# Two of VectorE's three exponential patterns, summed by accumulating DMAs and multiplied once

## The chip, the core and the metric

The kernel runs on one core of a Trainium2 chip. TensorE (PE), ScalarE (ACT), VectorE (DVE), GpSimd (POOL) and SyncE (SP) each work through an instruction list of their own, in order, and wait for one another by semaphores. The metric is the device time of one execution in microseconds, 644.52 for the kernel before (median of 3 runs, 644.18 to 644.57).

## What is computed

Two attention blocks over 2048 positions of width 512, with 32 heads of 16. Block A is linear attention, block B softmax attention; their outputs stand side by side.

```
# A
pq, pk = phi(q), phi(k)              # phi(t) = where(t > 0, t + 1, exp(t)) + 1e-6
num = pq @ (pk^T v);  den = pq @ sum(pk)
a = (num / den) @ wo
# B
p = softmax(q k^T / 4)               # per head, 2048 x 2048
b = (p @ v) @ wo
out = concatenate([a, b], axis=-1)
```

Nearly all the work is B's: 32 heads times 2048 x 2048 exponentials.

## The kernel before

**Tiling.** B goes in 32 *units*: four groups of eight heads (`Gp`), four chunks of 512 queries (`c`), two parities (`e_`), with four heads (`g`) in each unit. A unit has 64 *blocks*; a block is one head, 128 keys (`j`) and 512 queries. For each block TensorE makes the scores (`qk`, L946; four heads share the array, 32 rows each), an engine makes the exponentials, and TensorE multiplies them with V and a column of ones (`pv_cand`, L1355; four heads share the array, 32 columns each) into one PSUM bank per unit. The last unit does the same in halves of 256 queries (L943, L1348). Then VectorE transposes and normalizes (L1394 to L1410) and the output projection follows.

**Two ways to an exponential.** Most blocks go to ScalarE: two or three blocks of scores lie in the PSUM tile pS and one activation (L1161) writes them as f16 into PT, 25 slots. The other blocks lie in single banks of pD, pPV or pS, and VectorE turns them into f16 bit patterns with one multiply and add that writes int16 (L1065): the integer is read as an f16 and grows like the exponential, in straight pieces. To even out the pieces three such patterns are used, the second and third being the first plus 328 and plus 656. GpSimd makes those two with one integer add each (L1245) over a *group* of two blocks. The first pattern is multiplied with VX, which is V times 1.5547, the other two with VV, which is V: three PV products for a block of VectorE's, against one for a block of ScalarE's.

**Buffers.** The patterns lie in `DI`: 8 buffers (`NDG`), each for one group, with its three patterns one behind the other. A buffer comes free when all PV products of its group are done (`dgleft`, `dgfree`).

**What sets the order.** The program is written by a planner that runs while the kernel is built: it keeps a modelled time for each engine, lists of what may start, and picks the next instruction by start time and priority. `d_pick` chooses blocks for VectorE, `chain` hands a full group to GpSimd, `pv_cand` collects ready products into batches, and jobs of block A and the projections (L636, L735 and others) are put in between. A table `SEG` changes the planner's numbers about every 12 us of its own time, among them a seed for its choices among equals. On the chip only the order is left, with a semaphore wait wherever one instruction needs another's result or its buffer. So TensorE's next score product stands behind every PV product that the planner put ahead of it.

`Sched.add` records an instruction with what it reads and writes and derives its waits; a DMA has a lane (a semaphore) of its own and is issued by the queue that it is given, in that engine's order. A DMA also waits for the one before it on its lane.

Of the kernel before, what the change touches and what calls it, by code (L numbers as in the profile page):

```python
# [10 lines left out]
F16 = mybir.dt.float16  # L11
I16 = mybir.dt.int16
# [227 lines left out]
def bass_concat_heads__linear_attn_block__softmax_full_mha__prompt_kernel(nc, A_x, A_wqkv, A_wo, B_x, B_wqkv, B_wo, out):  # L240
# [8 lines left out]
    LAY = (25, 8)  # L249
    PW = 0.5  # L250
# [6 lines left out]
    NDG = LAY[1]  # L257
# [105 lines left out]
    JB = True  # L363
    WARM = (30, 6)
    HQ = 7.5
    TRACE = None
    PEB = 14


# [1433 lines left out]
```

## Time and profile before

| | |
|---|---|
| runs, median (lowest, highest) | 644.52 us (644.18, 644.57) |
| the profiled execution | 644.23 us |
| its span, first to last instruction | 642.5 us |
| TensorE clock granted | 0.998 |
| ScalarE, 655 exponentials | 615.4 us busy |
| VectorE, 722 pattern instructions, 723 blocks | 193.5 + 159.1 + 135.0 us busy |
| GpSimd, 726 integer adds | 433.2 us busy |
| DMA, all queues | 21.80 MB, 34 GB/s over the span |

The span is one execution as the profiler saw it. A line of the page names the source line, the engine, the operation, the tile written and the tiles read, then the count, the busy time and the mean length of one. The lengths of neighbours overlap on every engine, since a record ends when the result has been written and the next instruction starts before that; for the pace of an engine compare starts. PEld are the weight loads of the matmuls. A wait names who waited and whose instruction ended the wait.

### The profile page before, as it was taken

The numbers are of one execution on the slowest core, as the hardware profiler recorded it, in microseconds if no ns is written. First come the engines' busy times: TensorE is split into PE (matmuls) and PEld (weight loads), VectorE is DVE, ScalarE is ACT, GpSimd is POOL, SyncE is SP. The second block draws the span as 40 slices with busy tenths as digits, with TensorE's granted clock in tenths as the row PEclk, the third lists the DMA queues.
The fourth block names the chain that finished last, engine by engine and source line by source line (L and its number), as shares of the span: only waits on it lengthen the run. The fifth ranks groups of instructions, "written<-read, shape, count | busy, mean of one in ns | idle before, by whom it ended". The sixth has DMA issues, their size and how long they took to land.

```text
span 642.5 us, 20026 instructions
## 1 busy us (share of the span) xinstructions
PE 635.4 (99%) x8562; PEld 218.1 (34%) x8562; DVE 612.0 (95%) x1086; ACT 628.7 (98%) x692; POOL 440.5 (69%) x751
## 2 busy tenths in 40 slices
PE   8999999999999999999999999999999999999997
PEld 6333332333333333343333333223222322223243
DVE  6999999999999999999999999999999999999985
ACT  6999999999999999999999999999999999999995
POOL 4666788876767766657767676677776668766751
PEclk9999999999999999999999999999999999999999
DMA  9701000002010011012021012002110110000112
GB/s 187 209 2 24 21 1 12 8 3 43 3 35 1 2 35 35 10 35 45 18 50 51 3 41 45 17 10 50 28 34 10 27 34 18 26 11 26 35 43 71
DMA packets 53230, 21.80 MB, mean 34 GB/s; under 512 B 44176, under 2 KB 52624, under 8 KB 53136
## 3 DMA queue, kind: packets, MB, share of 16 engines
q1 hardware_dynamic: 51664, 19.80, 13.3%
q8 instruction: 69, 1.13, 0.7%
q10 hardware_dynamic: 1472, 0.66, 0.4%
q14 instruction: 25, 0.20, 0.1%
HBM read 4.46 MB, written 4.19 MB: 13 GB/s over the span
## 4 chain that ended last, share of the span: by engine, by line
PE 68%; ACT 31%; DVE 1%; issue 0%
ACT PT L1161 30%; PE pS L946 22%; PE pD L1355 20%; PE pD L636 7%; PE pPV L1355 4%; PE pS L636 4%; PE pPV L636 3%; PE pD L735 1%; PE pS L943 1%; ACT EA L751 1%; PE pD L946 1%; PE pD L1479 1%; PE pS L735 1%; PE pPV L946 0%; PE pD L1348 0%; PE pPV L1348 0%
## 5 line engine op out<-in xcount | busy, mean ns | idle before, releaser
L1161 ACT ACTIVATE PT<-pS 128x1024 f16<-128x1024 f32 (+1 forms) x655 | 615.4, 1082 | 1.3 <-PE pS L946 1.0
L1245 POOL INT64_ADD DI<-DI x726 | 433.2, 610 | 187.5 <-DVE DI L1065 184.2
L946 PE MATMUL pS<-QT,KM 32*128 32x512 bf16 x1512 | 255.1, 384 | 1.4 <-ACT PT L1161 0.5
L1065 DVE TENSOR_SCALAR DI<-pD 128x512 int16<-128x512 f32 (+1 forms) x288 | 193.5, 681 | 6.9 <-PE pD L946 2.1
L1355 PE MATMUL pD<-PT,VV 128*17 128x512 f16 x979 | 178.0, 381 | 0.0
L1355 PE MATMUL pD<-DI,VV 128*17 128x512 f16 x1114 | 176.8, 381 | 0.0
L1065 DVE TENSOR_SCALAR DI<-pS 128x512 int16<-128x512 f32 x235 | 159.1, 677 | 2.1 <-PE pS L946 1.3
L946 PEld LDWEIGHTS pS<-QT,KM 32*128 32x128 bf16 x1512 | 65.2, 91 | 231.3 <-ACT PT L1161 191.9
L1065 DVE TENSOR_SCALAR DI<-pPV 128x512 int16<-128x512 f32 x199 | 135.0, 678 | 4.6 <-PE pPV L946 2.5
L1355 PE MATMUL pD<-DI,VX 128*17 128x512 f16 x557 | 129.2, 382 | 0.0
L946 PE MATMUL pD<-QT,KM 32*128 32x512 bf16 x275 | 102.8, 384 | 0.0
L946 PE MATMUL pPV<-QT,KM 32*128 32x512 bf16 x197 | 75.7, 384 | 0.0
L1355 PE MATMUL pPV<-PT,VV 128*17 128x512 f16 x299 | 52.0, 381 | 0.0
L1355 PEld LDWEIGHTS pD<-DI,VV 128*17 128x17 bf16 x1114 | 38.9, 88 | 33.6 <-issue 22.3
L1355 PEld LDWEIGHTS pD<-PT,VV 128*17 128x17 bf16 x979 | 39.0, 88 | 30.5 <-issue 24.9
L1355 PE MATMUL pPV<-DI,VV 128*17 128x512 f16 x298 | 49.3, 381 | 0.0
L1355 PEld LDWEIGHTS pD<-DI,VX 128*17 128x17 bf16 x557 | 28.5, 88 | 17.9 <-issue 14.4
L1355 PE MATMUL pPV<-DI,VX 128*17 128x512 f16 x149 | 34.2, 382 | 0.0
L946 PEld LDWEIGHTS pD<-QT,KM 32*128 32x128 bf16 x275 | 24.3, 90 | 1.9 <-DVE DI L1065 0.7
L946 PEld LDWEIGHTS pPV<-QT,KM 32*128 32x128 bf16 x197 | 17.8, 90 | 1.9 <-DVE DI L1065 1.4
L636 PE MATMUL pD<-Wa,xTa 128*32 128x256 bf16 x448 | 18.1, 275 | 0.0
L636 PE MATMUL pS<-Wa,xTa 128*32 128x256 bf16 x448 | 18.0, 275 | 0.0
(202 smaller groups left out, 534.1 us busy)
## 6 DMA issues: line engine op xcount, KB each, us to landing
out_dram<-KNa SPq DMA_DIRECT2D x31, 128.0 KB, 1.8
Wa<-in_A_wqkv_dram SPq DMA_DIRECT2D x1, 1536.0 KB, 8.7
KM<-KR SPq DMA_DIRECT2D x96, 16.0 KB, 1.8
Wb<-in_B_wqkv_dram SPq DMA_DIRECT2D x2, 384.0 KB, 5.6
Wb<-in_B_wqkv_dram SPq DMA_DIRECT2D x1, 512.0 KB, 4.6
Wa<-in_A_wo_dram SPq DMA_DIRECT2D x1, 512.0 KB, 4.4
Wa<-in_B_wo_dram SPq DMA_DIRECT2D x1, 512.0 KB, 3.7
ON<-in_B_x_dram ACTq DMA_DIRECT2D x1, 256.0 KB, 2.8
```

The source lines that it names most:

```text
L636: ins = self.e.matmul(out_[32 * g:32 * g + 32], lhsT=lhsT[:, 32 * g:32 * g + 32], rhs=rhs, start=start, stop=stop, tile_position=(0, 32 * g))
L735: return e.matmul(f32v(bk)[:, tl * 128:(tl + 1) * 128], lhsT=xTb[:, cc, t * 128:(t + 1) * 128], rhs=Wb[:, cc, 1024 + Gp * 128:1024 + Gp * ...
L751: ("act", 0.0635 + n * 0.000833, f_ev("act", lambda e, bk: e.activation(EA[:, 0:n], f32v(bk)[:, c0:c0 + n], ACTF.Exp), [], ["EA"])),
L943: ins = e.matmul(dst[:, 256 * i:256 * i + 256], lhsT=KM[32 * g:32 * g + 32, Gp % 2, e_, (2 * jp + i) * 128:(2 * jp + i + 1) * 128], rhs=QT ...
L946: return e.matmul(dst, lhsT=KM[32 * g:32 * g + 32, Gp % 2, e_, j * 128:(j + 1) * 128], rhs=QT[32 * g:32 * g + 32, Gp % 2, c * 512:(c + 1) ...
L1065: sch.add("dve", lambda e, db_=DBANK[b0]: e.tensor_scalar(DI[:, di_at(0, buf) + i * 512:di_at(0, buf) + (i + n) * 512], f32v(db_, n * 512) ...
L1161: sch.add("act", lambda e: e.activation(PTf[:, p0 * 512:p0 * 512 + w], S5[:, c0:c0 + w], ACTF.Exp, scale=SC), reads=skeys(sl, len(bl)), wr ...
L1245: sch.add("pool", lambda e, v=v, word=word: e.int64_add(at64(v), at64(0), word), reads=keys, writes=[("DI", v, x) for x in best])
L1355: sch.add("pe", lambda e, g=g, j=j, c0=c0, V_=V_, r2=r2, P=P, first=first, last_=last_, pb_=pvb[0]: e.matmul(pb_[0][32 * g:32 * g + 17, pb ...
L1479: ins = e.matmul(f32v(wb_, 128), lhsT=ZW[:], rhs=ZW[:], start=True, stop=True)
```

## The change

It has four parts.

1. After GpSimd's two adds a DMA issued by GpSimd adds the third pattern onto the second, as f16 (`accum_op=ALU.add`). The sum is multiplied with VV once, so a block of VectorE's takes two PV products. A group is left as it was, with three products, when the planner's GpSimd backlog is too long or the last unit is near its end (`joined`). There are 273 such DMAs: 197 over one group (two blocks) and 76 over two groups (four blocks), on six lanes in turn.
2. The three patterns lie in three planes with slots of their own, 9, 9 and 6, 24 as before. A slot of the first plane comes free after its VX products and GpSimd's adds, one of the third when the DMA has landed.
3. GpSimd may join two groups in one add (and one DMA) whatever their slots. The way by which VectorE made the later patterns itself in the last unit is gone.
4. The table `SEG` is new, so all orders are new.

The core of the diff:

```diff
-    LAY = (25, 8)
-    PW = 0.5
+    LAY = (25, (9, 9, 6))
+    PW = 0.8
...
-        (12.0,0.05,5,3.0,0,2,6,4,9.5,26,2.5,7.0,0.8,1.8,3,7.0,1.5,2.5,1.5,3,1,0.3,6,0,-9.0,2,1.2,0,55),
+        (12.1089,0.05,5,3.0,0,2,6,4,9.5,26,2.5,7.0,0.8,1.8,3,7.0,1.5,2.5,1.5,3,1,0.3,6,0,-9.0,2,1.2,0,55),
...
+    PDM = 6.0
+    DMT = 30
+    PDF = 0.58
+    PDG = 0.4
+    SDL = 2.0
+    SDB = 0.00137
+    SDM = 1.3
+    NSL = 6
...
-        DIR = 3 * DGW
-        DI = sb("DI", [128, NDG * DIR], I16)
+        DI = sb("DI", [128, sum(NPL) * DGW], I16)
 
         def di_at(v, b):
 
-            return b * DIR + v * DGW
+            return (sum(NPL[:v]) + b) * DGW
...
+        def plane_hold(v, b, n):
+
+            pfree[v][b] = None
+            pusers[v][b] += n
+
+        def plane_done(v, b, t):
+
+            pusers[v][b] -= 1
+            plast[v][b] = max(plast[v][b], t)
+            if pusers[v][b] == 0:
+                pfree[v][b] = plast[v][b]
+                plast[v][b] = 0.0
...
+        sum_lanes = [sch.new_dma_lane() for _ in range(NSL)]
...
+                joined = p_backlog(st_) < PDM and not (u_min(items) == NU - 1 and left[NU - 1] < DMT)
+                for v in (1, 2):
+                    for x in slots[v]:
+                        plane_hold(v, x, 1 if joined and v == 2 else n)
                     word = int.from_bytes(struct.pack("<4H", *[SHIFT[v - 1]] * 4), "little")
-                    sch.add("pool", lambda e, v=v, word=word: e.int64_add(at64(v), at64(0), word), reads=keys, writes=[("DI", v, x) for x in best])
+                    sch.add("pool", lambda e, v=v, word=word: e.int64_add(at64(v), at64(0), word), reads=keys, writes=[("DI", v, x) for x in slots[v]])
                     T["pool"] = st_ = st_ + PFX + len(best) * w * PEL
...
+                if joined:
+                    lane = sum_lanes[nsum[0] % len(sum_lanes)]
+                    nsum[0] += 1
+                    sch.add(lane, lambda e: e.dma_start(at16(1), at16(2), accum_op=ALU.add), reads=[("DI", 2, x) for x in slots[2]], writes=[("DI", 1, x) for x in slots[1]], queue="pool")
+                    T["pool"] = st_ + PDF + (len(best) - 1) * PDG
+                    sum_end[0] = max(st_ + SDL, sum_end[0]) + len(best) * w * SDB
+                    land = sum_end[0] + SDM
+                    for x, it in zip(slots[1], items):
+                        for b in it:
+                            pv_due[b[0]][b[2]] -= 1
+                            if b[0] == LU:
+                                half_due[b[1] // 8][b[2]] -= 1
+                        give(x, it, 1, land)
+                    for x in slots[2]:
+                        plane_done(2, x, land)
```

In the lines of the kernel after, L953 is the score product, L1401 the PV product, L1195 the exponential, L1096 VectorE's pattern, L1277 the integer add and L1287 the accumulating DMA.

What moves, first on GpSimd. These are its rows before, from the end of the start-up work on; an ISA row is an integer add, its 128x512 are 1024 int16 of two blocks.

```order
L532 AFFINE_SELECT BMk<-BMk 128x128
L547 MEMSET VNa 128x32
L1245 ISA DI<-DI 128x512 x510
L1245 ISA DI<-DI 128x256 x2
L1245 ISA DI<-DI 128x512 x6
```

And these are its rows now, from the middle of the program, with what each waits for: s_dve is VectorE's semaphore, s_pool GpSimd's own, s_d29 and the like are lanes of the accumulating DMAs.

```order
L1277 ISA DI<-DI 128x2x512
L1287 DMA DI<-DI 128x2x1024 [waits s_pool]
L1277 ISA DI<-DI 128x1024 [waits s_dve]
L1277 ISA DI<-DI 128x1024 [waits s_d34,s_d29]
L1287 DMA DI<-DI 128x2048 [waits s_pool]
L1277 ISA DI<-DI 128x512 [waits s_dve]
L1277 ISA DI<-DI 128x512 [waits s_d30]
L1287 DMA DI<-DI 128x1024 [waits s_pool]
```

A DMA stands behind each pair of adds and waits for them; the second add of a pair, into the third plane, waits for an earlier DMA to have landed. Pairs over two groups stand among those over one.

On TensorE, in the seventeenth unit, this is a batch of PV products before, with the score products and half a V projection (L735) behind it; DI,VX is a first pattern, DI,VV a second or third, PT a block of ScalarE's.

```order
L1355 MATMUL pPV<-DI,VV 17x512 x4
L1355 MATMUL pPV<-PT,VV 17x512
L1355 MATMUL pPV<-DI,VX 17x512
L1355 MATMUL pPV<-PT,VV 17x512 x2
L946 MATMUL pS<-QT,KM 128x512 x2
L946 MATMUL pD<-QT,KM 128x512
L735 MATMUL pS<-Wb,xTb 128x128 x8
```

And this stands near the start of the same unit now.

```order
L953 MATMUL pPV<-QT,KM 128x512
L1401 MATMUL pD<-DI,VX 17x512 x2
L1401 MATMUL pD<-PT,VV 17x512 x2
L953 MATMUL pS<-QT,KM 128x512 x2
L953 MATMUL pD<-QT,KM 128x512
L1401 MATMUL pD<-PT,VV 17x512
L1401 MATMUL pD<-DI,VV 17x512 x3
```

The unit has 110 PV products before and 88 now, its batches are shorter, and of DI,VV there is one for a block instead of two.

More of the change, by code (lines that the diff above doesn't have):

```diff
@@ L256, in bass_concat_heads__linear_attn_block__softmax_full_mha__prompt_kernel @@
     DG = 2
-    NDG = LAY[1]
+    NPL = LAY[1]
     VW = 1.5546875
@@ L978, in bass_concat_heads__linear_attn_block__softmax_full_mha__prompt_kernel, with plane_pick, plane_gate @@
         dgroup = {"n": 0, "buf": 0, "open": False}
-        dgfree = [0.0] * NDG
-        dgleft = [0] * NDG
+        pfree = [[0.0] * n for n in NPL]
+        dgfree = pfree[0]
+        pusers = [[0] * n for n in NPL]
+        plast = [[0.0] * n for n in NPL]
+        def plane_hold(v, b, n):
[7 more added lines that the diff above has]
+                plast[v][b] = 0.0
+        def plane_pick(v, n, t):
+            fr = sorted((x, b) for b, x in enumerate(pfree[v]) if x is not None)[:n]
+            return sorted(b for x, b in fr) if len(fr) == n and fr[-1][0] <= t else None
+        def plane_gate():
+            g = [min((x for x in pfree[v] if x is not None), default=None) for v in (1, 2)]
+            return None if None in g else max(g)
         def cur_unit():
@@ L1016, in d_pick @@
             if not dgroup["open"]:
-                buf = min((i for i in range(NDG) if dgfree[i] is not None), key=lambda i: (dgfree[i] > at, (i - dgroup["buf"] - 1) % NDG), default=None)
+                buf = min((i for i in range(NPL[0]) if dgfree[i] is not None), key=lambda i: (dgfree[i] > at, (i - dgroup["buf"] - 1) % NPL[0]), default=None)
                 if buf is None or dgfree[buf] > at:
@@ L1033, in d_take @@
                 dgroup["n"] += 1
-                dgfree[buf] = None
-                dgleft[buf] = 0
+                plane_hold(0, buf, 1)
                 dgroup["st"][buf] = {"taken": 0, "closed": False, "items": []}
@@ L1038, in d_take @@
             s_["taken"] += 1
-            dgleft[buf] += 3
+            plane_hold(0, buf, 1)
             if s_["taken"] == DG:
@@ L1072, in p1 @@
                         dfree[x] = en_ + LPE["dve"]
-                        pv_ready[b_[0]].append((en_ + LPE["dve"], b_, (DI.bitcast(F16)[:, di_at(0, buf) + k_ * 512:di_at(0, buf) + (k_ + 1) * 512], ("DI", 0, buf, k_)), ("d", buf), "X"))
+                        pv_ready[b_[0]].append((en_ + LPE["dve"], b_, (DI.bitcast(F16)[:, di_at(0, buf) + k_ * 512:di_at(0, buf) + (k_ + 1) * 512], ("DI", 0, buf, k_)), ("d", 0, buf), "X"))
                     s_["t"] = en_
@@ L1079, in bass_concat_heads__linear_attn_block__softmax_full_mha__prompt_kernel @@
         pshift = []
+        nsum, sum_end = [0], [0.0]
+        sum_lanes = [sch.new_dma_lane() for _ in range(NSL)]
+        DF = DI.bitcast(F16)
         pv_give = {}
@@ L1203, in chain, with give @@
             s_["chained"] = True
-            late = left[NU - 1] < DE3 and all(b[0] == NU - 1 for b in s_["items"])
             n = len(s_["items"])
             w = 512 * n
-            rk = [("DI", 0, buf, i) for i in range(n)]
-            def give(buf_, v, lane, en_):
-                for i, b in enumerate(dgroup["st"][buf_]["items"]):
-                    P = DI.bitcast(F16)[:, di_at(v, buf_) + i * 512:di_at(v, buf_) + (i + 1) * 512]
-                    pv_ready[b[0]].append((en_ + (LPE["pool"] if lane == "pool" else LPE["dve"]), b, (P, ("DI", v, buf_)), ("d", buf_), "V"))
-            def plain(v):
-                def run(st_, en_):
-                    sch.add("dve", lambda e: e.tensor_scalar(DI[:, di_at(v, buf):di_at(v, buf) + w], DI[:, di_at(0, buf):di_at(0, buf) + w], 1.0, float(SHIFT[v - 1]), op0=ALU.mult, op1=ALU.add),
-                            reads=rk, writes=[("DI", v, buf)])
-                    give(buf, v, "plain", en_)
-                return run
+            def give(slot, items, v, t):
+                for i, b in enumerate(items):
+                    P = DI.bitcast(F16)[:, di_at(v, slot) + i * 512:di_at(v, slot) + (i + 1) * 512]
+                    pv_ready[b[0]].append((t, b, (P, ("DI", v, slot)), ("d", v, slot), "V"))
             def on_pool(st_, en_):
-                near_ = {x[1]: x for x in pshift if x[2] == w and x[3][0] <= st_ + PMW}
+                near_ = {x[0]: x for x in pshift if x[1] == w and x[2][0] <= st_ + PMW}
                 near_[buf] = me[0]
                 best = [buf]
-                for step in range(1, NDG):
-                    run_ = [buf]
-                    while len(run_) < JN and run_[-1] + step in near_:
-                        run_.append(run_[-1] + step)
-                    while len(run_) < JN and run_[0] - step in near_:
-                        run_.insert(0, run_[0] - step)
-                    if len(run_) > len(best):
-                        best = run_
-                keys = []
+                for b2 in sorted(near_, key=lambda b2: near_[b2][2][0]):
+                    if b2 != buf and len(best) < JN and plane_pick(1, 2, st_) and plane_pick(2, 2, st_):
+                        best = sorted((buf, b2))
+                keys, items = [], []
                 for b_ in best:
@@ L1237, in on_pool @@
                     if b_ != buf:
-                        cands["pool"].remove(x[3])
-                        st_ = max(st_, x[3][0])
+                        cands["pool"].remove(x[2])
+                        st_ = max(st_, x[2][0])
                     keys += [("DI", 0, b_, i) for i in range(n)]
-                at64 = lambda v: bass.AP(DW, DW[:, di_at(v, best[0]) // 4:].offset, [list(DW[:, 0:1].ap[0])] +
-                                         ([[(best[1] - best[0]) * DIR // 4, len(best)]] if len(best) > 1 else []) + [[1, w // 4]])
@@ L1243, in on_pool, with at64, at16 @@
-                for v in vs:
+                    items.append(dgroup["st"][b_]["items"])
+                slots = [best] + [plane_pick(v, len(best), st_) for v in (1, 2)]
+                def at64(v):
+                    sl = slots[v]
+                    return bass.AP(DW, DW[:, di_at(v, sl[0]) // 4:].offset, [list(DW[:, 0:1].ap[0])] +
+                                   ([[(sl[1] - sl[0]) * DGW // 4, 2]] if len(sl) > 1 else []) + [[1, w // 4]])
+                def at16(v):
+                    sl = slots[v]
+                    return bass.AP(DF, DF[:, di_at(v, sl[0]):].offset, [list(DF[:, 0:1].ap[0])] + ([[(sl[1] - sl[0]) * DGW, 2]] if len(sl) > 1 else []) + [[1, w]])
@@ L1246, in on_pool @@
                     T["pool"] = st_ = st_ + PFX + len(best) * w * PEL
-                    for x in best:
-                        pv_give[x, v](st_)
-            vs = (1, 2)
-            if late:
-                for v in vs:
-                    push("dve", s_["t"], -2, 0.06 + w * 0.00027, plain(v))
-                return
-            for v in vs:
-                pv_give[buf, v] = lambda en_, v=v: give(buf, v, "pool", en_)
-            me = [(vs, buf, w, push("pool", s_["t"] + LTO["dve", "pool"], 0, len(vs) * (PFX + w * PEL), on_pool), rk)]
+                    if not joined:
+                        for x, it in zip(slots[v], items):
+                            give(x, it, v, st_ + LPE["pool"])
@@ new lines, in on_pool @@
+                for x in best:
+                    plane_done(0, x, st_ + LPE["pool"])
+                if joined:
[13 more added lines that the diff above has]
+                        plane_done(2, x, land)
@@ L1257, in chain, with u_min @@
+            def u_min(items):
+                return min(b[0] for it in items for b in it)
+            me = [(buf, w, push("pool", s_["t"] + LTO["dve", "pool"], 0, 2 * (PFX + w * PEL), on_pool))]
             pshift.append(me[0])
@@ L1362, in run @@
                     if src[0] == "d":
-                        dgleft[src[1]] -= 1
-                        if dgleft[src[1]] == 0 and dgroup["st"][src[1]]["closed"]:
-                            dgfree[src[1]] = en
+                        plane_done(src[1], src[2], en)
                     else:
@@ L1639, in bass_concat_heads__linear_attn_block__softmax_full_mha__prompt_kernel @@
             opts = []
+            gate = plane_gate()
             for eng in T:
                 best = None
+                if eng == "pool" and gate is None:
+                    continue
                 for c_ in cands[eng]:
-                    st = max(pe_at("v" if isinstance(c_[3], Rounds) else "j") if eng == "pe" else T[eng], c_[0])
+                    st = max(pe_at("v" if isinstance(c_[3], Rounds) else "j") if eng == "pe" else T[eng], c_[0], gate if eng == "pool" else 0.0)
                     k_ = (round(st / 0.05), c_[1], c_[2])
```

104 rows, old and new, of the table SEG are left out of this document.

## The prediction

> **What bounds the kernel now.** I read the page first, for the load of each engine and the chain, then the waits, then ScalarE's timeline, and last one late step of it.
>
> ```profile
> span 642.5 us, 20026 instructions
> PE 635.4 (99%) x8562; PEld 218.1 (34%) x8562; DVE 612.0 (95%) x1086; ACT 628.7 (98%) x692; POOL 440.5 (69%) x751
> PE 68%; ACT 31%; DVE 1%; issue 0%
> ```
>
> Three engines look full, and the chain goes through TensorE and ScalarE alone. The profiled execution took 644.23 us, 1.73 more than its span; the median of the runs, 644.52, lies 0.29 above it. A step that I cost at x us in the span I take off the median as it stands.
>
> ```profile
> PEld pS L946 <- ACT PT L1161: 191.9, 481, 0.6
> POOL DI L1245 <- DVE DI L1065: 184.2, 220, 5.3
> PEld pD L1355 <- POOL DI L1245: 5.5, 23, 0.4
> ```
>
> The columns are us in total, times, longest. A fill of the score banks pS (L946) waits for ScalarE to have read a bank 481 times. There are 655 exponentials, so in some 174 cases the bank was free and TensorE came later. GpSimd mostly waits for work, and TensorE hardly waits for GpSimd. "Busy" hides the rest: an exponential is recorded for 1072 ns, but the next starts before it ends. So I take the distance of starts.
>
> ```profile
> 504.18 13.85 ACT L1161 ACTIVATE PT<-pS 128x1024 f16<-128x1024 f32 x15
> 515.92 3.02 ACT L1161 ACTIVATE PT<-pS 128x1024 f16<-128x1024 f32 x3
> 8.51 34.81 ACT L1161 ACTIVATE PT<-pS 128x1536 f16<-128x1536 f32 x36 [0.97 <-PE pS L946]
> 444.88 0.69 ACT L751 ACTIVATE EA<-pPV 128x512 bf16<-128x512 f32 x1
> 445.36 39.29 ACT L1161 ACTIVATE PT<-pS 128x1024 f16<-128x1024 f32 x42
> 484.53 0.61 ACT L751 ACTIVATE EA<-pPV 128x512 bf16<-128x512 f32 x1
> 633.44 1.02 ACT L1161 ACTIVATE PT<-pS 128x1024 f16<-128x1024 f32 x1
> L1161 ACT ACTIVATE PT<-pS 128x1024 f16<-128x1024 f32 x640 | 597.4, 1072 | 0.3
> L1161 ACT ACTIVATE PT<-pS 128x1536 f16<-128x1536 f32 x15 | 22.5, 1497 | 1.0 <-PE pS L946 1.0
> ```
>
> The first two rows are one tight stretch seen in two windows: its 14th exponential starts at 515.92, so 13 steps take 11.74 us, 0.903 each. That is ScalarE's own speed for two blocks; a third block adds 1497 - 1072 = 425 ns. From 445.36 to 484.53 it is 39.17 / 42 = 0.933. Over the whole kernel: 633.44 - 8.51 = 624.9 us between the first and the last start. The work in it is 639 x 0.903 + 15 x 1.328 + 32 x 0.48 (the EA steps: 445.36 - 444.88) = 612.3. **So 12.6 us are lost in steps too long by a little each, 0.07 us in each of the 174.** Here is one:
>
> ```profile
> 445.36 2.99 ACT L1161 ACTIVATE PT<-pS 128x1024 f16<-128x1024 f32 x3
> 446.14 0.39 PE L1355 MATMUL pD<-PT,VV 128*17 128x512 f16 x2
> 446.58 0.38 PE L1355 MATMUL pD<-DI,VV 128*17 128x512 f16 x2
> 446.90 0.39 PE L946 MATMUL pS<-QT,KM 32*128 32x512 bf16 x2
> 447.33 1.02 ACT L1161 ACTIVATE PT<-pS 128x1024 f16<-128x1024 f32 x1
> ```
>
> Three exponentials start from 445.36 on; the third at 447.33, so the first two steps take 1.97, where 1.81 would do. TensorE was in a batch of twelve PV products from 446.14 to 446.90, and the fill came 0.43 before the start. What ends last is TensorE's batch, not ScalarE.
>
> **The change part by part.** *PV products taken out.*
>
> ```profile
> L1355 PE MATMUL pD<-DI,VV 128*17 128x512 f16 x1114 | 176.8, 381 | 0.0
> L1355 PE MATMUL pPV<-DI,VV 128*17 128x512 f16 x298 | 49.3, 381 | 0.0
> 489.44 1.19 PE pD L1355 x20
> 494.94 0.76 PE pD L1355 x12
> ```
>
> The 1412 products of the second and third pattern become 716 in the new order, 696 fewer: there are 273 sums, 197 of two blocks and 76 of four, 698 blocks in all, a few of them in the last unit, whose products are counted apart. Eight products more cost 1.19 - 0.76 = 0.43 us, so one costs 0.054 and the whole is 37.5 us of TensorE. Most of it is worth nothing, as ScalarE stands beside it with 612 us of its own; it can win back the 12.6 us at most. Which share? The late fills stand behind long batches. In the two orders I count the stretches between two groups of score products that hold at least twelve PV products: 88 before, 61 now, 31% fewer. I take 0.31 x 12.6 = **3.9 us**, with 0 and 12.6 as ends.
>
> *Split of the blocks.* ScalarE goes from 640 two-block and 15 three-block exponentials to 633 and 18, and one of a single block: 7 x 0.903 less, 3 x 1.328 and 0.48 more, **1.9 us less**; VectorE goes from 723 to 727 blocks.
>
> ```profile
> L1065 DVE TENSOR_SCALAR DI<-pD 128x512 int16<-128x512 f32 x287 | 192.3, 679 | 6.9 <-PE pD L946 2.1 <-PE pD L943 2.0 <-PE pPV L946 0.7
> ```
>
> Four times 0.68 is 2.7 us, inside VectorE's 30 us of idle span; 2.7 if that cover were gone.
>
> *GpSimd's integer adds and DMA issues.*
>
> ```profile
> L1245 POOL INT64_ADD DI<-DI x726: 397/611/636, 16.4 to 631.4; - x182
> 299.52 1.20 POOL L1245 INT64_ADD DI<-DI  x2 [0.59 <-DVE DI L1065]
> 302.88 3.59 POOL L1245 INT64_ADD DI<-DI  x6 [0.15 <-DVE DI L1065]
> 300.00 1.23 SPq L682 DMA_DIRECT2D KM<-KR  x2
> 301.27 1.83 SPq L485 DMA_TRANSPOSE xTa<-in_A_x_dram  x1
> 638.83 0.38 ACTq L1471 DMA_DIRECT2D out_dram<-KNa  x1
> ```
>
> An add over two blocks costs (3.59 - 1.20) / 4 = 0.598 us; half the width is 611 - 397 = 214 ns shorter, so double width is about 1.03. Now there are 422 of the first and 152 of the second kind: 252 + 157 = 409 us, 25 less than now. On top stand 273 DMA issues, each behind a wait for the add before it, and in the queue behind it stand the next groups' adds, for which TensorE waits. No DMA is issued by GpSimd in this trace. The nearest rows are the issues of other queues: 0.38 (ScalarE's), 0.62 (SP's plain copy, 1.23 for two), 1.83 (SP's transpose). I take 0.62, the plain copy of the busiest queue: 169 us, 578 together. GpSimd's work runs from 16.4 to 632, 616 us long and 610 after the gain, so it fits with 32 us to spare and costs nothing; the other ends are 513 and 909.
>
> The Trainium skill, in "DMA: Bandwidth & Descriptors" (SWDGE vs HWDGE vs iDMA), says that GpSimd writes its descriptors into SBUF by software and that VectorE shuts it out of there while it runs in a two-port mode. The adds do not show such a lock: 611 in the median, 636 at most, beside VectorE's whole program. By the row it costs nothing, and by the rule at most VectorE's fast SBUF steps.
>
> *The sum itself.* It lands between the adds and the one product that now stands for two.
>
> ```profile
> out_dram<-KNa SPq DMA_DIRECT2D x31, 128.0 KB, 1.8
> ON<-in_B_x_dram ACTq DMA_DIRECT2D x1, 256.0 KB, 2.8
> Wa<-in_A_wo_dram SPq DMA_DIRECT2D x1, 512.0 KB, 4.4
> Wa<-in_A_wqkv_dram SPq DMA_DIRECT2D x1, 1536.0 KB, 8.7
> GB/s 187 209 2 24 21 1 12 8 3 43 3 35 1 2 35 35 10 35 45 18 50 51 3 41 45 17 10 50 28 34 10 27 34 18 26 11 26 35 43 71
> ```
>
> In the orders I count exponentials between a group's score product and the first product with its third pattern (before) or its sum (now): median 6 before and 10 now, least 3 and 7. Four more at 0.92 give 3.7 us for issue and landing. Two blocks are 256 KB, 2.8 by the row of that size; with 0.62 for the issue 3.4, which just fits. Four blocks would take 4.4 + 0.62 = 5.0; these 76 have a median of 11. So no wait is left by the rows, and the bounds are a gain of nothing and the loss in the second rival. In bulk, 698 x 128 KB is 91 MB in 610 us, 150 GB/s; the slices at the start moved 187 and 209, the wide load 177 (1536 KB in 8.7). It fits if the sum costs no more than a copy.
>
> *Planes and orders.* 24 slots remain 24, in three planes; a slot of the third plane is held until the sum lands, and adds now wait for that, on GpSimd's queue: again nothing while it has its 32 us. Start and tail (8.5 before the first exponential, 8.0 after the last) keep their steps; I cost them at 0.
>
> **Sum:** -3.9 - 1.9 = -5.8; span 636.7, run 638.4 by the profile, **638.7** against the median.
>
> **The rivals.**
>
> *GpSimd becomes the bound (slower).* Place: its in-order queue from 16.4 us on. It decides where an issue, with the wait ahead of it, costs more than (610 - 409) / 273 = 0.74 us; at 0.8 it is 409 + 218 = 627, and with 16.4 ahead and 10.5 behind 654, as a run 656. For it: the rows reach to 1.83, and the work is near the limit at the nearest row already. Against: the nearest row is below. At 1.0 the work is 682, the span 709, the run 711. "DMA: Bandwidth & Descriptors" (Latency and other measured facts) of the Trainium skill gives about 1 us to GpSimd's first byte, as the cost of writing the descriptors; if all of that held the queue, its time would be this 711. No run here shows it, and only part of a latency need occupy the engine.
>
> *The sums land late (slower).* Place: the PV product on the sum, behind which TensorE's next fill stands. It decides beyond 3.7 us from adds to landing. A group's loop is ten exponentials, 9.3 us; 0.2 us over in it is 2.2%, 13 us of 610, so 652. For it: a sum reads two operands where a copy reads one, and 150 GB/s is 72% of the best slice before the transposes and loads that come in between. Against: four exponentials were put between.
>
> *TensorE's relief is hidden (same).* The 174 late fills wait for something else than PV batches (a bank still held by VectorE, a group of projection products); then only the split counts, and small new waits eat it: 643.2 to 645.8.
>
> *ScalarE at its own speed (faster by more).* All 12.6 come back: 644.5 - 14.5 = 630.0, with up to 3 us left standing 633.
>
> **How the numbers follow.** A measurement of this kernel tells about 0.2%, 1.3 us, from no change. My case, 634 to 643.2: 0.52. ScalarE at its own speed: 0.08. Hidden relief: 0.12. GpSimd bound: 0.15, of which 0.03 for 1 us or more an issue. Late sums: 0.13. That is faster 0.60, same 0.12, slower 0.28. The range is to leave out a fifth: below 631 some 0.04, above 658 the heavy half of the two slower cases, 0.14; so 631 to 658, around a likeliest case of 634 to 643.
>
> **What would show it.** Right: starts of exponentials nearer 0.91 than 0.923 apart in the mean, fewer long steps behind batches of twelve, GpSimd at 85 to 95% with issues of about 0.6, and hardly any wait of L1401 for a DMA. Wrong: GpSimd without gaps and VectorE's banks waiting behind it (first rival); PV weight loads that wait for a DMA of DI, and DMA slices near full (second); a mean distance still at 0.923 with TensorE idle elsewhere (third). An issue over 0.74 us breaks the forecast, whatever else holds.

## The result and the profile after

The kernel after takes 801.75 us in the median of four runs (799.22 to 805.92), the one before 644.43 beside it (644.18 to 644.57): a ratio of 1.245, with an interval of 1.239 to 1.251. That is 157 us slower, and 144 us above the top of the range. The profiled execution is the slowest of the four, 805.92.

The page, for the load of the engines and the chain:

```profile
span 804.2 us, 18808 instructions
PE 686.0 (85%) x7884; PEld 218.6 (27%) x7884; DVE 629.8 (78%) x1091; ACT 644.6 (80%) x689; POOL 684.8 (85%) x874
POOL 70%; PE 10%; issue 9%; DMA 6%; DVE 3%; ACT 0%; POOLq 0%
POOL DI L1277 44%; POOL DI L1287 26%; DMA DI<-DI 6%; PE pS L953 2%; DVE DI L1096 2%; PE pPV L1401 1%; PE pD L1401 1%; PE pD L643 1%; PE pD L1394 1%; PE pS L950 1%; PE pS L643 1%; PE pD L742 1%; PE pS L742 0%; PE pD L1523 0%; PE pPV L1394 0%
```

No engine is at 98% any more, and the chain that went through TensorE and ScalarE now goes through GpSimd's adds (L1277) and its DMAs (L1287). GpSimd shows only 85% busy. What it does in the rest is told by its groups, with the idle time before them, and by the waits.

```profile
L1277 POOL INT64_ADD DI<-DI x576 | 499.9, 1052 | 14.7 <-DVE DI L1096 14.6
L1287 POOL DMA_DIRECT2D DI<-DI x273 | 255.6, 936 | 86.4 <-POOL DI L1277 82.2
```

```profile
PEld pD L1401 <- DMA DI<-DI: 83.1, 63, 4.1
POOL DI L1287 <- POOL DI L1277: 82.2, 269, 1.0
ACT PT L1195 <- PE pS L953: 74.8, 68, 6.1
PE pD L1401 <- DMA DI<-DI: 61.9, 49, 3.8
```

GpSimd waits for VectorE for 14.6 us in all, where it did for 184 before. Its other wait is for itself: 269 times a DMA waits 0.3 us for the end of the adds just ahead of it. So its queue is full nearly from end to end. TensorE waits for sums and ScalarE for TensorE; the experiments show that these waits are consequences. A few consecutive groups of two blocks on GpSimd give the price of one sum:

```profile
306.41 1.50 POOL L1277 INT64_ADD DI<-DI  x2
308.23 0.87 POOL L1287 DMA_DIRECT2D DI<-DI  x1 [0.31 <-POOL DI L1277]
308.83 1.51 POOL L1277 INT64_ADD DI<-DI  x2
310.64 0.87 POOL L1287 DMA_DIRECT2D DI<-DI  x1 [0.30 <-POOL DI L1277]
311.25 1.51 POOL L1277 INT64_ADD DI<-DI  x2
```

From DMA to DMA it is 310.64 - 308.23 = 2.41 us. Two adds alone take 2 x 0.588 = 1.18, by the starts of such pairs. **A sum therefore costs 1.23 us of the queue:** its record of 0.87, the wait of 0.30, and 0.06 by which the two adds behind it end later after it than they would behind an add (308.23 + 0.87 = 309.10, the pair ends at 310.34, 1.24 later and not 1.18). The next adds start 0.6 after the DMA, inside its record, but they end only behind it: the distance of starts hides the 0.87, the ends show it.

```profile
L1287 POOL DMA_DIRECT2D DI<-DI x273: 867/873/1229, 18.0 to 777.5; - x137
L1277 POOL INT64_ADD DI<-DI x576: 401/931/1537, 16.5 to 789.4; - x192
q0 software_dynamic: 45584, 91.51, 66.3%
DI<-DI POOLq DMA_DIRECT2D x197, 256.0 KB, 3.8
DI<-DI POOLq DMA_DIRECT2D x76, 512.0 KB, 5.1
```

The DMAs have two lengths. The longest, 1.2, are those of two groups whose slots don't adjoin, 49 of the 273 in the order; the other 224 move one piece in each partition and take 0.87. So GpSimd has 403 us of adds (422 x 0.588 + 152 x 1.015 and two halves) and 224 x 1.24 + 49 x 1.57 = 355 of sums. Before its first add lie 16.5 us, and 5.4 of the 14.6 us of waits for VectorE are among these; so 9.2 of waits remain behind it, with 3.6 ahead of two DMAs for which the profile names no cause. From its last add (789.4) to the end it is 14.8. Together that is 802 of the span's 804.

### The profile page after: what moved, and what is told of

The parts are those of the page before. It is cut to its first block, busy times and chain, and to the rows that moved or that the text cites. A ratio compares the mean times of both kernels' runs of the same rounds, so it can differ in the third digit from the quotient of the medians.

```text
span 804.2 us, 18808 instructions
## 1 busy us (share of the span) xinstructions
PE 686.0 (85%) x7884; PEld 218.6 (27%) x7884; DVE 629.8 (78%) x1091; ACT 644.6 (80%) x689; POOL 684.8 (85%) x874
## 3 DMA queue, kind: packets, MB, share of 16 engines
q0 software_dynamic: 45584, 91.51, 66.3%
q1 hardware_dynamic: 51664, 19.80, 12.6%
## 4 chain that ended last, share of the span: by engine, by line
POOL 70%; PE 10%; issue 9%; DMA 6%; DVE 3%; ACT 0%; POOLq 0%
POOL DI L1277 44%; POOL DI L1287 26%; DMA DI<-DI 6%; PE pS L953 2%; DVE DI L1096 2%; PE pPV L1401 1%; PE pD L1401 1%; PE pD L643 1%; PE pD L1394 1%; PE pS L950 1%; PE pS L643 1%; PE pD L742 1%; PE pS L742 0%; PE pD L1523 0%; PE pPV L1394 0%
## 5 line engine op out<-in xcount | busy, mean ns | idle before, releaser
L1195 ACT ACTIVATE PT<-pS 128x1024 f16<-128x1024 f32 (+1 forms) x652 | 629.8, 1050 | 143.6 <-PE pS L953 74.8
L1277 POOL INT64_ADD DI<-DI x576 | 499.9, 1052 | 14.7 <-DVE DI L1096 14.6
L1287 POOL DMA_DIRECT2D DI<-DI x273 | 255.6, 936 | 86.4 <-POOL DI L1277 82.2
L953 PE MATMUL pS<-QT,KM 32*128 32x512 bf16 x1499 | 273.8, 413 | 5.0 <-ACT PT L1195 3.6
L1096 DVE TENSOR_SCALAR DI<-pD 128x512 int16<-128x512 f32 x323 | 218.4, 684 | 65.0 <-PE pD L953 45.2
L1096 DVE TENSOR_SCALAR DI<-pS 128x512 int16<-128x512 f32 x224 | 152.6, 681 | 23.7 <-PE pS L953 23.1
L1096 DVE TENSOR_SCALAR DI<-pPV 128x512 int16<-128x512 f32 x180 | 122.8, 682 | 36.2 <-PE pPV L953 17.3
L1401 PE MATMUL pD<-PT,VV 128*17 128x512 f16 x898 | 149.4, 421 | 0.3 <-ACT PT L1195 0.3
L1401 PE MATMUL pD<-DI,VV 128*17 128x512 f16 x520 | 91.0, 415 | 63.7 <-DMA DI<-DI 61.9
L953 PEld LDWEIGHTS pS<-QT,KM 32*128 32x128 bf16 x1499 | 64.7, 92 | 239.7 <-ACT PT L1195 135.4
L953 PE MATMUL pD<-QT,KM 32*128 32x512 bf16 x315 | 124.5, 409 | 1.3 <-DVE DI L1096 0.9
L1401 PE MATMUL pD<-DI,VX 128*17 128x512 f16 x510 | 117.3, 431 | 0.0
L953 PE MATMUL pPV<-QT,KM 32*128 32x512 bf16 x170 | 68.5, 403 | 0.4 <-DVE DI L1096 0.2
L1401 PE MATMUL pPV<-DI,VV 128*17 128x512 f16 x196 | 35.1, 420 | 34.6 <-DMA DI<-DI 34.5
L1401 PE MATMUL pPV<-PT,VV 128*17 128x512 f16 x380 | 59.0, 409 | 0.0
L1401 PEld LDWEIGHTS pD<-DI,VV 128*17 128x17 bf16 x520 | 19.7, 89 | 106.2 <-DMA DI<-DI 83.1
L1401 PE MATMUL pPV<-DI,VX 128*17 128x512 f16 x196 | 44.6, 425 | 0.0
L1401 PEld LDWEIGHTS pD<-PT,VV 128*17 128x17 bf16 x898 | 30.8, 90 | 34.8 <-issue 29.5
L953 PEld LDWEIGHTS pD<-QT,KM 32*128 32x128 bf16 x315 | 27.8, 91 | 10.5 <-DVE DI L1096 6.9
L1438 DVE STREAM_TRANSPOSE pD<-pD 128x512 f32<-128x512 f32 x22 | 16.0, 727 | 16.2 <-PE pD L1401 16.1
L1401 PEld LDWEIGHTS pD<-DI,VX 128*17 128x17 bf16 x510 | 23.5, 91 | 18.1 <-issue 15.2
L1401 PEld LDWEIGHTS pPV<-DI,VV 128*17 128x17 bf16 x196 | 7.6, 89 | 49.9 <-DMA DI<-DI 45.7
```

The lines of the kernel that those rows point to most:

```text
L953: return e.matmul(dst, lhsT=KM[32 * g:32 * g + 32, Gp % 2, e_, j * 128:(j + 1) * 128], rhs=QT[32 * g:32 * g + 32, Gp % 2, c * 512:(c + 1) ...
L1096: sch.add("dve", lambda e, db_=DBANK[b0]: e.tensor_scalar(DI[:, di_at(0, buf) + i * 512:di_at(0, buf) + (i + n) * 512], f32v(db_, n * 512) ...
L1195: sch.add("act", lambda e: e.activation(PTf[:, p0 * 512:p0 * 512 + w], S5[:, c0:c0 + w], ACTF.Exp, scale=SC), reads=skeys(sl, len(bl)), wr ...
L1277: sch.add("pool", lambda e, v=v, word=word: e.int64_add(at64(v), at64(0), word), reads=keys, writes=[("DI", v, x) for x in slots[v]])
L1287: sch.add(lane, lambda e: e.dma_start(at16(1), at16(2), accum_op=ALU.add), reads=[("DI", 2, x) for x in slots[2]], writes=[("DI", 1, x) fo ...
L1401: sch.add("pe", lambda e, g=g, j=j, c0=c0, V_=V_, r2=r2, P=P, first=first, last_=last_, pb_=pvb[0]: e.matmul(pb_[0][32 * g:32 * g + 17, pb ...
```

## Experiments

Three theories stood against one another. **Q**: GpSimd's in-order queue pays for each sum, and its work no longer fits. **T**: the transfers, or the landing of the sums, make TensorE wait. **O**: the new orders are slow whatever a sum costs. Each kernel was run and profiled once, with a run of the kernel before on the same chip: 644.33, 645.01, 644.75 and 644.64 us in the four groups. The kernel before thus varies by 0.8 us and the kernel after by 6.7; single times that differ by less, near 644 and near 800, are taken as equal. All edits are of the kernel after, whose profiled execution (805.92) is the one compared. The last columns show when ScalarE's last instruction starts and how long the span goes on behind it.

| kernel | time, us | a sum of one piece costs GpSimd | GpSimd waits for VectorE | last start on ScalarE | span behind it |
|---|---|---|---|---|---|
| before | 644.23 | - | 184 | 638.2 | 4.3 |
| after | 805.92 | 0.30 + 0.87 + 0.07 | 14.6 | 795.2 | 9.0 |
| no sums | 643.19 | - | 204.6 | 637.3 | 4.2 |
| thin sums | 802.09 | 0.30 + 0.87 + 0.07 | 6.0 | 794.6 | 5.7 |
| copy by SP | 664.23 | - | 221.0 | 658.2 | 4.2 |
| copy by GpSimd | 707.11 | 0.30 + 0.55 + 0.07 | 11.6 | 695.3 | 10.1 |
| 16 rows | 754.14 | 0.29 + 0.77 + 0.07 | 9.4 | 745.9 | 6.5 |
| late issue | 787.81 | 0 + 0.85 + 0.07 | 88.9 | 777.0 | 9.0 |
| half of the sums | 662.44 | 0.30 + 0.87 + 0.07 | 53.4 | 653.3 | 7.4 |
| never joined | 658.12 | - | 222.5 | 652.0 | 4.3 |
| true price | 691.25 | 0.30 + 0.87 + 0.07 | 38.2 | 681.5 | 7.9 |
| late, planned | 727.51 | 0 + 0.85 + 0.07 | 30.3 | 715.5 | 10.2 |
| between | 758.01 | 0 + 0.85 + 0.07 | 60.5 | 746.9 | 9.4 |
| late and thin | 728.73 | 0 + 0.85 + 0.07 | 30.8 | 721.2 | 5.6 |
| half, thin | 652.39 | 0.30 + 0.87 + 0.07 | 37.5 | 641.7 | 9.0 |
| quarter | 650.98 | 0.30 + 0.87 + 0.07 | 124.1 | 640.1 | 9.1 |

### No sums

```diff
-                    sch.add(lane, lambda e: e.dma_start(at16(1), at16(2), accum_op=ALU.add), ..., queue="pool")
```

> The order of the changed kernel with the 273 accumulating DMAs left out; the third pattern is then missing from the result. Theory Q (GpSimd's queue is the bound: each DMA costs it 1.24 us, since a single group takes 2.42 us from add to add in the changed kernel and two adds alone 1.18): without them GpSimd has about 415 us of adds, no longer binds, and the time falls to 630 to 648. Theory T (the sums' transfers and their landing bind): the same, 630 to 648. Theory O (the new orders are bad in themselves, DMA or not): it stays over 680.

643.19 us: the whole loss is the sums', and O falls. But even with the sums for nothing the new orders gain only 1.1 us, little more than the 0.8 by which the kernel before varies. From the page, the groups by form and ScalarE's timeline:

```profile
PE 622.8 (97%) x7882; PEld 215.1 (34%) x7884; DVE 612.9 (96%) x1091; ACT 626.6 (98%) x689; POOL 416.1 (65%) x601
L1277 POOL INT64_ADD DI<-DI x576 | 408.8, 723 | 212.0 <-DVE DI L1096 204.6
```

```profile
L1195 ACT ACTIVATE PT<-pS 128x1024 f16<-128x1024 f32 x633 | 590.4, 1078 | 2.5 <-PE pS L953 1.5 <-PE pD L953 0.7
L1195 ACT ACTIVATE PT<-pS 128x1536 f16<-128x1536 f32 x18 | 26.5, 1471 | 1.0 <-PE pS L953 1.0
8.78 2.37 ACT L1195 ACTIVATE PT<-pS 128x1536 f16<-128x1536 f32 x2 [0.97 <-PE pS L953]
629.66 5.18 ACT L1195 ACTIVATE PT<-pS 128x1024 f16<-128x1024 f32 x5
```

The last exponential, the one of a single block and 0.59 long, ends at 634.84 and so starts at 634.25, 625.5 after the first. The work in between is 633 x 0.903 + 18 x 1.328 + 32 x 0.48 = 610.9. So 14.6 us are lost in long steps, where the kernel before lost 12.6: in these orders, taking 696 products from TensorE gave ScalarE nothing back.

### Thin sums, and plain copies by SP and by GpSimd

```diff
# thin: 32 columns
-    ... + [[1, w]])
+    ... + [[1, 32]])
# copy by SP; the copy by GpSimd is the same with queue="pool"
-    e.dma_start(at16(1), at16(2), accum_op=ALU.add), ..., queue="pool")
+    e.dma_start(at16(1), at16(2)), ..., queue="sp")
```

In the copies the third pattern takes the place of the sum.

> The same 273 accumulating DMAs, from the same queue, over all 128 partitions, but over 32 of the 1024 columns of each slot, so one row is 64 bytes and not 2 KB and all of them move 2.9 MB where 91.5 were moved; the rest of the third pattern is left out of the sum. Theory Q: the cost is in making and issuing, not in the bytes, so GpSimd's cycle stays at 2.4 us for a group and the time at 755 to 800. Theory T: with the bytes gone it falls to 630 to 670.

> The sums become plain copies of the same bytes and are issued by SP's queue in place of GpSimd's (a copy overwrites the second pattern with the third, so the second is missing from the result). Theory Q: GpSimd is left with its adds, the bytes still move, and the time falls to 630 to 690, the upper end if SP's queue holds its other transfers up. Theory T: the transfers still land at 4 us and more and fill the DMA engines, so it stays over 740.

> The sums become plain copies of the same bytes, still issued by GpSimd; the second pattern is missing from the result. Theory Q: nothing changes on GpSimd's queue, 770 to 805, with shorter landings only. Theory T, where the accumulation's second read is the price: 680 to 740.

Thin sums, the queue of the DMAs, its records and the landing:

```profile
q0 software_dynamic: 49040, 2.88, 11.0%
L1287 POOL DMA_DIRECT2D DI<-DI x273: 865/871/1229, 18.2 to 779.1; - x137
L1287 POOL DMA_DIRECT2D DI<-DI x273 | 264.2, 968 | 87.5 <-POOL DI L1277 82.0
DI<-DI POOLq DMA_DIRECT2D x197, 8.0 KB, 2.0
```

2.9 MB are moved and not 91.5, a sum lands in 2.0 us and not 3.8, and the time is 802.09, about as before the edit and just above Q's band. So the loss is not the bytes, and T falls for this kernel. The edit also changes something else: 32 columns of two slots never adjoin, so all 76 sums over two groups have two pieces and not 49 (the mean record is 968 ns, where it was 936). That is 27 x 0.33 = 9 us more on GpSimd. Against it stand 8.6 us less of waits for VectorE and some 4 less at the end. So by these sums the bytes cost the kernel after at most some 13 of its 157 us. The DMA's record on GpSimd for one piece is the same for 8 KB and for 256: it is no transfer time. The Trainium skill's "Perfetto Trace Analysis" (DMA Instruction — SWDGE (GPSIMD)) says that such a record ends when the last of two of GpSimd's processors has written its descriptors, and not when the data is moved; this pair of runs agrees.

With the copies issued by SP, GpSimd is as in the kernel without sums:

```profile
L1277 POOL INT64_ADD DI<-DI x576 | 409.4, 725 | 232.3 <-DVE DI L1096 221.0
```

The time is in Q's band, and 142 us are gone. The 21 above the kernel without sums are a loss of its own: some 10 us in the first 40, where SP also issues the loads and transposes, and some 4 at 440 to 480. What of it is SP's queue and what the landing was not separated. That only GpSimd's DMAs can add on the way is what the Trainium skill's "DMA: Bandwidth & Descriptors" (SWDGE vs HWDGE vs iDMA) states; no run here shows it. That is why this kernel copies.

The copy by GpSimd came out at 707.11, in the band that theory T had named and far below Q's 770 to 805. But its timeline shows why, and it is not the transfers:

```profile
304.09 0.56 POOL L1287 DMA_DIRECT2D DI<-DI  x1 [0.30 <-POOL DI L1277]
304.69 2.06 POOL L1277 INT64_ADD DI<-DI  x2
307.05 0.72 POOL L1287 DMA_DIRECT2D DI<-DI  x1 [0.30 <-POOL DI L1277]
```

The wait is still 0.30, but the record is 0.56 for one piece and 0.72 for two, and not 0.87 and 1.20. A sum thus costs GpSimd 0.32 or 0.48 more than a copy: 224 x 0.32 + 49 x 0.48 = 95 us, and 99 were measured. Q had taken the price for one of any DMA; it is that of an accumulating one.

### 16 rows

```diff
-    list(DF[:, 0:1].ap[0])
+    list(DF[0:16, 0:1].ap[0])
```

> The accumulating DMA takes in 16 of the 128 partitions, all columns of them; the sum is missing in the other 112 rows, so the output is not the reference's. As many DMAs, queues and waits as in the changed kernel. Theory Q (GpSimd's queue pays some 1.24 us for each sum): if what it pays is the writing of a descriptor for each row, an eighth of the rows costs an eighth, 0.16 us, GpSimd has 409 + 43 = 452 us of work and the time falls to 643 to 655. If it pays a fixed price for each DMA, the record stays at 0.87 and the time at 795 to 806. In between, the fixed part is read from the record and from the distance to the next add. Theory T (transfers): an eighth of the bytes, as the thin kernel had a thirty-second; nothing new, 800.

```profile
311.06 0.77 POOL L1287 DMA_DIRECT2D DI<-DI  x1 [0.29 <-POOL DI L1277]
311.62 1.46 POOL L1277 INT64_ADD DI<-DI  x2
313.37 0.77 POOL L1287 DMA_DIRECT2D DI<-DI  x1 [0.29 <-POOL DI L1277]
```

754.14 is the expectation's case in between. An eighth of the rows takes 0.10 off the record of one piece and 0.39 off that of two (0.82 in the median): 224 x 0.10 + 49 x 0.39 = 42 of the 52 us. Most of the price belongs to the DMA and not to its rows.

### Late issue, and late with thin sums

```diff
+        held_sum = []
...
                     T["pool"] = st_ = st_ + PFX + len(best) * w * PEL
...
+                flush_sums()
...
-                    sch.add(lane, lambda e: e.dma_start(...), ..., queue="pool")
+                    issue = lambda: sch.add(lane, lambda e: e.dma_start(...), ..., queue="pool")
+                    held_sum.append((issue, slots))
# late and thin: also
-    ... + [[1, w]])
+    ... + [[1, 32]])
```

> Everything is computed. A sum's DMA is issued after the two adds of the next group (or before its product, where that comes first), so that the add it waits for has long ended; the sum lands some 2 us later. Theory Q: the wait of 0.30 us for GpSimd's own add goes, and with it what a DMA loses behind the end of the add ahead of it, 0.32, if that is not work. One DMA then costs between 0.605 and 0.94 us of the queue, GpSimd has 409 + 165 to 257 = 574 to 666 us, and with 27 us at the ends and up to 30 of other waits the time is 650 to 725, against 802. If the whole 1.24 us are work of GpSimd, nothing moves: 795 to 810. Theory T (late landing is what counts): later sums make it slower, 805 to 850.

> The late issue with 32 of a sum's 1024 columns, 2.9 MB instead of 91.5; the sum is missing in the others, so the output is not the reference's. In the late issue the sums landed 4.9 us after the issue and the DMA engines were busy for eight or nine tenths. If that is what makes the products late, the landing falls to some 2 us and the time to 720 to 760. If it is the place of the DMA in GpSimd's queue (behind adds that wait for VectorE), 780 to 790.

GpSimd in the thin one:

```profile
302.89 2.87 POOL L1296 DMA_DIRECT2D DI<-DI  x1
304.85 2.16 POOL L1285 INT64_ADD DI<-DI  x2
306.00 1.87 POOL L1296 DMA_DIRECT2D DI<-DI  x1
307.34 2.62 POOL L1285 INT64_ADD DI<-DI  x2
309.34 1.46 POOL L1296 DMA_DIRECT2D DI<-DI  x1
```

No wait stands ahead of the DMAs, and the records have grown, since an instruction now starts while earlier ones are still at work. So one reads the ends. They are 305.76, 307.01, 307.87, 309.96, 310.80: a pair of adds 1.25 after a DMA, a DMA 0.86 after a pair, a double pair 2.09 after that, a DMA 0.84 after it. The wait was 0.30 of the 1.24, and the other 0.92 are work that GpSimd can't do beside its adds. By that the thin kernel, with its 76 sums of two pieces, has 403 + 197 x 0.92 + 76 x 1.24 = 678 us of work. With 16.6 ahead, 25.3 of waits for VectorE behind the first add and 11.5 behind the last it is 732, 5 more than its span of 726.9. The time, 728.73, is in the band for late landing.

With whole sums the late issue is 59 us longer: 787.81, which lies in none of the bands named for it. Landing, from the start of the record, and waits there:

```profile
DI<-DI POOLq DMA_DIRECT2D x197, 256.0 KB, 4.9
POOL DI L1285 <- DVE DI L1096: 88.9, 71, 5.5
PEld pD L1413 <- DMA DI<-DI: 73.9, 68, 3.3
```

GpSimd has 9 us less of work here, as 49 sums and not 76 have two pieces, but it waits 88.9 us for VectorE, which waits for TensorE, which waits for sums. These are issued a group later. The 4.9 us, where it was 3.8, are no slower landing, since the records now begin earlier: from the end of the record a sum lands in 3.7 us in the median here, in 3.5 in the kernel after, and in 1.3 in the thin one. Late issue and whole bytes together make the products wait. Here T is right, as the second limit behind the first.

### Between, and late with a plan for it

```diff
# between: flush_sums() after the next group's first add
+                    if v == 1:
+                        flush_sums()
# late, planned: the late issue, and
-    PDF = 0.58
-    PDG = 0.4
-    SDL = 2.0
+    PDF = 0.6
+    PDG = 0.1
+    SDL = 4.5
```

> Everything is computed, the changed kernel's orders on all engines but GpSimd. As the late issue, but the DMA stands between the two adds of the next group, one add earlier. The wait for GpSimd's own add should be gone here too (one add lies between), so the queue pays 0.57 to 0.70 for a sum, and the sum is issued 0.6 to 1.0 us sooner than in the late issue. If lateness made its 788, 700 to 770; if GpSimd's price did, no more than the late issue's: 785 to 795.

> Everything is computed. As the late issue, but the planner is told that a sum lands 2.5 us later and that an issue costs 0.6, so that it puts the products of the sums later: 277 sums (224 and 53), ScalarE 621 and 33. GpSimd: 479 x 0.59 + 114 x 1.03 = 400 us of adds, 277 x 0.57 to 0.70 = 158 to 194 of sums, no bound. Theory Q with lateness as the second limit: the late issue alone (788) lost by products that come before their sums, so the time falls to 650 to 680. If it stays above 740, it is not the place of the products that lost there.

Between came at 758.01, in the band for lateness and 30 us below the late issue, with the same work on GpSimd and 60.5 us of waits for VectorE: one add sooner is worth that. The planned one came at 727.51, below the 740 above which the place of the products would not have mattered, but not at 650 to 680. The expectation had priced a sum at 0.57 to 0.70, by the distance of starts; at 0.92 and 1.24 it is about 400 us of adds and 270 of sums, so GpSimd was still the bound (665 us busy of a span of 726).

### Half of the sums, half and thin, a quarter

```diff
+                    if nsum[0] % 2 == 0:       # quarter: % 4
                         sch.add(lane, lambda e: e.dma_start(...), ..., queue="pool")
```

> Every second accumulating DMA is left out (136 of 273 stay); for the others the third pattern is missing, so the output is not the reference's. TensorE has the same products. Theory Q: GpSimd has 409 + 136 x 1.24 = 578 us of work, less than the 610 at which it would bind, and the time falls most of the way to the kernel without DMAs: 645 to 665. A loss in proportion to the number (643 + 159 / 2 = 722) would speak for a price of each sum that no other work can hide, that is for late landing (T).

> Every second sum left out as in the kernel with half of the sums, and of those left 32 of 1024 columns; the output is not the reference's. GpSimd's work is as with half of the sums (584 us), the landing falls from 3.6 us to about 2. Theory Q (a nearly full queue): the time stays at 658 to 663. Theory T (what is left there is late landing): it falls by most of the 19 us, to 643 to 650.

> Only every fourth sum is issued (69 of 273), whole; the third pattern is missing elsewhere, so the output is not the reference's. GpSimd has 409 + 69 x 1.3 = 499 us of work, over 100 below the bound. Theory Q: a queue with that much slack costs next to nothing, 643 to 647. Theory T: each sum costs its landing, a quarter of the sums half of what half of them cost: 652 to 655.

Half of the sums gave back 143 us, and 662.44 is in Q's band. So the loss is not in proportion to the number: it comes with GpSimd's work passing what the rest takes. But 19 stayed against the kernel without sums, in two parts. Behind ScalarE's last instruction the span goes on for 7.4 and not 4.2 us, and up to there it is 16.0 longer. With thin sums (652.39, between the two bands) these 16.0 are 4.4, with a quarter of the sums 2.8. So some 12 of the 16 are the transfers' (T), though GpSimd's 579 us of work fit; some 5 of the 12 are lost in one place, at the start, where the loads and transposes run. The waits of the half kernel from 10 to 50 us:

```profile
ACT PT L1195 <- PE pD L953: 5.2, 1, 5.2
DVE DI L1096 <- PE pD L953: 5.1, 2, 4.9
PEld pPV L1402 <- DMA DI<-DI: 5.0, 1, 5.0
```

One sum holds up TensorE for 5 us, and ScalarE and VectorE behind it; with thin sums that wait is not there. The quarter's 650.98 lies above Q's 643 to 647 and below T's 652 to 655. Up to ScalarE's end Q is right, 2.8 us; what it missed is the end: all kernels with DMAs from GpSimd end later behind ScalarE (5.6 to 10.2 us, the others 4.2 or 4.3). In the trace GpSimd's last DRAIN takes 3.6 us there, 4.8 in the kernel after and 0.05 in the kernels without such DMAs.

### Never joined, and the planner with the true price

```diff
# never joined
-                joined = p_backlog(st_) < PDM and not (...)
+                joined = False
# true price
-    PDM = 6.0
-    PDF = 0.58
-    PDG = 0.4
+    PDM = 3.0
+    PDF = 1.24
+    PDG = 0.17
```

> No group is joined: no DMA, three products for each block as before, everything computed; the planes, the joining of two groups in one add and the new table stay (the planner makes new orders from them). It shows what some 696 PV products are worth beside the kernel without DMAs (643.2). If TensorE's batches cost what the forecast said (3.9 us), 646 to 650; if TensorE, at 99% in the kernel before, is a bound that the sums had lifted, up to 655; if the products are worth nothing, 642 to 645.

> Everything is computed. The planner is told the measured price of a sum (1.24 us of GpSimd, 0.17 more for a second slot) and joins a group only while its backlog there is below 3 us: 176 sums are left (111 over two blocks, 65 over four), and ScalarE gets more blocks (607 exponentials of two blocks and 44 of three). Theory Q: GpSimd has 409 x 0.59 + 146 x 1.03 = 391 us of adds and 176 x 1.3 = 229 of sums, 620, and 647 with its ends; ScalarE has 622 us of work, 16.5 around it and some 13 lost, 652. So 650 to 665, still slower than before. Theory T (each sum costs by its landing): 643 + 176 / 273 x 159 = 745. Theory O (the new orders are bad in themselves) can't tell.

Never joined: 658.12, above all its bands, and for a reason that the expectation didn't have. The planner gave ScalarE 614 exponentials of two blocks and 44 of three, 17 us more work than without sums; by the starts only 11.5 us are lost in its long steps, with about 1,400 products on second and third patterns. So it does not show what the products are worth; with twice as many of them, in other orders, the lost time was not longer. The true price: 691.25, above the 650 to 665. GpSimd has about the 620 us of work that I had counted, 94% of the time from its first add to its last, and waits 38.2 for VectorE beside them. That it is fed in bursts would explain these waits; it was not tested. No version that computes everything came out faster than the kernel before.

## Why the prediction was wrong

**The step that failed** is GpSimd's integer adds and DMA issues: "I take 0.62, the plain copy of the busiest queue: 169 us, 578 together ... so it fits with 32 us to spare and costs nothing." The adds were right: 409 us forecast, 403 by the distance of starts. A sum costs 1.24 us, and 1.57 where it has two pieces: 355 us and not 169. Three things stand against the 0.62. SP's row is the issue of another queue and bounds nothing on GpSimd; that a plain copy there, without its wait, comes to 0.55 + 0.07 = 0.62 as well is chance. The accumulating form takes 0.87 + 0.07. And the wait of the DMA for the adds ahead of it, which the text named, was given no price: 0.30, a quarter of the whole. The measured 1.24 lies halfway from the 0.62 to the upper bound of 1.83, so the bounds held and the choice between them did not.

**The first rival** was right in its mechanism and its place, and its point of decision fits. It decides above 0.74 us an issue, that is above 610 us of work; a quarter and half of the sums lie below that load and stay within 20 us of the kernel without, the whole lies above and costs 157. Its price stopped at 1.0 us, 711. By its formula with 355 us of sums the time is 409 + 355 + 16.4 + 10.5 + 1.7 = 793; the waits for VectorE and the longer end make the rest. The rule that I set beside it, from the Trainium skill's "DMA: Bandwidth & Descriptors" (Latency and other measured facts), gives about 1 us to the first byte. The accumulating DMA of one piece comes near it, with 0.92 us of work on GpSimd; the plain copy, with 0.55 + 0.07, does not. My doubt whether GpSimd is held for most of such a time was misplaced for the accumulating form.

**The 3.9 us of TensorE's relief** came to nothing even where the sums are free: 14.6 us are lost and not 8.7. The third rival, hidden relief with 643.2 to 645.8, comes nearest for the orders alone (643.19). The orders do hold fewer long batches, 61 and not 88, but the time lost in long steps did not fall with them; what the late fills wait for instead stays open, so the reason that the third rival gives is not shown.

**The split of the blocks** held: the counts of exponentials are the forecast ones, 1.9 us less of work. (612.3 before and 610.9 now differ by 1.4, because both leave out the last exponential, which was one of two blocks and is one of a single block.) VectorE's 2.7 us don't show in the time without sums.

**The landing** was sized nearly right (3.4 and 5.0 forecast from the issue, 3.8 and 5.1 measured). With the wait of 0.30 it is 4.1 from the adds, past the 3.7 at which the second rival was to decide, but in the kernel after it decides little: thin sums take about as long there. Nor do the adds wait for a landing that frees a slot: the trace of the kernel after has no such wait. In the other kernels it is a second limit, 59 us in the late issue and some 12 with half of the sums. The second rival was thus real, but stood behind the first.

**Start and tail at 0** missed 4.8 us at the end, GpSimd's last drain.

## What to carry to other kernels

Price a new instruction only by a row of the engine that will issue it; where there is none, let the point of decision set the chance: here it was 0.74 us between bounds of 0.38 and 1.83, and that is no case for 0.15. Count the wait of an instruction for the one just ahead of it on its own in-order engine: on GpSimd it was 0.30 us each time here, 82 us in all. And where instructions overlap, take an engine's price from the distance of ends in a stretch that never waits, not from starts.

## What the runs showed of the hardware

- GpSimd is held by a DMA that it issues, and the time does not depend on the bytes: 0.87 us for an accumulate of 128 rows, of 64 bytes or of 2 KB each, 1.20 for two pieces in each row, 0.77 for one piece of 16 rows; a plain copy 0.55 and 0.72. The adds behind it end 0.07 later still.
- An accumulating DMA is more than a copy elsewhere too: 45584 packets against 26704 for the same 273 transfers, and 256 KB land in 3.8 us against 2.5.
- After DMAs from GpSimd its last drain takes 1.7 to 6.3 us, and 0.05 without them; what it waits for no run shows.
- The granted clock of TensorE was lower in the runs in which it waits more: 0.90 in the kernel after, 0.957 with the copy by GpSimd, 0.995 without sums. The products with a second pattern or a sum are recorded at 415 ns in the kernel after and 381 before. GpSimd's own work accounts for the span without this; how much the clock adds no run separates.
